# A first expert layer in seven block products per unit, with the products chained in PSUM

## The chip, the core and the metric

The kernel runs on one core of a Trainium2 chip. Five engines work side by side, each through its own instructions in order: TensorE (PE in the profile; its weight loads are PEld), VectorE (DVE), ScalarE (ACT), GpSimd (POOL) and SyncE (SP), which here only issues transfers. The metric is the device time of one execution in microseconds (us), the median of several runs.

## What is computed

Attention with a computed position bias, then a dense layer pair with softplus between, then eight gated experts:

```
x  = attention(q, k, v, bias(w1, b1, w2))            # 1152 tokens x 512
h  = x @ w_in                                        # 512 x 2048, given as float64
x  = (max(h, 0) + log1p(exp(-abs(h)))) @ w_out       # 2048 x 512, float64
P  = exp(x @ w_gate - max); 8 times: normalise rows, then columns
out = sum over e of P[:, e] * (max(x @ w1[e], 0) @ w2[e])   # 8 x (512 x 1024, 1024 x 512)
```

## The kernel before

After the attention the program is a row of 40 *units*. A unit is 256 of the hidden columns of one layer: units 0 to 7 are the dense pair (called the first expert stage here, `u < U1`), units 8 to 39 the eight experts, four units each (the second stage). Every unit does the same work on TensorE, in this order:

- *up*: the 512 x 256 piece of the first matrix against 1024 tokens, the tokens in two blocks of 512 (c = 0, 1), the 256 columns in two blocks of 128 (f = 0, 1), so four results (c, f) of 128 x 512. `up_last` (L763 to L771) does the same for the last 128 tokens.
- the function between the layers (`act`: softplus on ScalarE in the first stage, ReLU in the second), whose result is split into a rounded part `h[:, 0]` (ScalarE) and the rest `h[:, 1]` (VectorE, L736 or L738).
- *down* (L782 to L800): the 256 x 512 piece of the second matrix against the result, for c = 0 in four sums, a pair of transposes (L776), c = 1 in four sums, and one more sum (L809). VectorE adds each sum to the accumulator (L826, or L828 with the gate's weight).

All operands are float32, split in two parts, and each product is three matmuls (`TRIPS`). So the weights of each unit are split as well: `high` (L639) writes the rounded part of the up weights (ScalarE, L636) and the rest (GpSimd, L637), and `highd` (L643) does so for the down weights. The weights of the first stage come as float64 words: four pieces of 128 x 512 in each unit go through `magnitude` (m: a VectorE mask, L601, then a clamp on GpSimd, L602), `convert_a` (a, L607), `convert_b` (b, L612) and `convert_c` (c, L618), on VectorE. The lists `CONVERT` and `JOBS` say at which places of unit u the weights of unit u + 1 are converted, mixed and split; everything goes to the engines in the order in which the Python code names it.

In the second stage (from unit 9) the four up results are not made from eight block products of 128 columns but from seven (`PRODUCTS`), by the Strassen-Winograd scheme: sums of blocks of the tokens (S1 to S4, made once, in unit 8), sums of blocks of the weights (T1 to T4, made by `mix`, L624 to L633, four GpSimd instructions in each unit, then split by a second `high`), seven products, and sums of products on VectorE (`after`, L745 to L761). A block product is six matmuls of 128 x 512 (L699); a plain result of the first stage (`plain`, L702 to L715) is twelve. Units 0 to 8 use `plain`.

PSUM has eight banks: four for the sums of *down* (two tiles of two banks), two under the tag "t", and one each under "tail" and "pv". The gate's small products, in units 8 to 12, take "pv" or "tail" in between (`gate`, asked for at named places).

Of the kernel before, what the change touches and what calls it, by code (L numbers as in the profile page):

```python
# [80 lines left out]
            7: ("S3", "T3")}  # L81
WAT = {"B11": 0, "B21": 512, "B22": 640, "T1": 1024, "T4": 1152, "T3": 1536, "T2": 1664}
# [10 lines left out]
def attention_moe_moe_kernel(ctx: ExitStack, tc, qT, kT, vN, wpos, w_in, w_out, w_gate, e_w1, e_w2,  # L93
# [439 lines left out]
    def experts(m0, accp, xr):  # L533
# [8 lines left out]
        NU = U1 + E * UE  # L542
        wide = w_in.dtype != F32
# [95 lines left out]
        def high(u, k):  # L639
            if u < NU and (u >= U1 or not k):  # L640
# [51 lines left out]
        def product(u, n):  # L692
            z[n] = bank({2: "tail", 5: "pv"}.get(n, "t"))
            xn, wn = PRODUCTS[n]
            k = 0
            for j in range(2):
                for a, b in TRIPS:
                    o = WAT[wn] + 256 * j
                    nc.tensor.matmul(z[n], wu(u)[:, a, o:o + 128], xs[xn][b][j], start=(k == 0), stop=(k == 5))  # L699
# [17 lines left out]
        def add(out, n, name):  # L717
            nc.vector.tensor_tensor(out=out, in0=z[n], in1=hold[name], op=ALU.add)  # L718
# [174 lines left out]
        def tokens_down(c):  # L893
            lt, m = bank("pv"), CHUNKS[c][1] // 128
# [11 lines left out]
        def max_all():  # L906
            mt = bank("pv")
# [3 lines left out]
        def exps():  # L911
            pool["mb"] = mb = bank("pv")
# [16 lines left out]
        def columns(it):  # L929
# [3 lines left out]
            def first():  # L933
                cs["t"] = t = bank("pv")
# [317 lines left out]
```

## Time and profile before

| what | us |
|---|---|
| median of 3 runs (1246.45 to 1248.13) | 1247.13 |
| the profiled execution | 1245.35 |
| its span, first to last instruction | 1243.5 |
| TensorE busy in it | 1186.5 |
| VectorE, GpSimd, ScalarE busy | 825.9, 554.8, 492.4 |

Read with it: the first expert stage lies between 261 and 473 us of the span (unit 1 begins at 295.3, unit 4 at 371.8, unit 5 at 397.3, unit 7 at 448.4), unit 8 ends at 506, and from 608 us on one unit follows another every 23.5 us. A busy TensorE is a modelled figure; how far it waits is read unit by unit, from the length of a unit.

### The profile page before, as it was taken

How to read it: one execution, taken by the hardware profiler on the slowest of the kernel's cores; microseconds unless marked ns; L12 is line 12 of the kernel's file. 1: busy time of each engine (PE TensorE's matmuls, PEld its weight loads, DVE VectorE, ACT ScalarE, POOL GpSimd, SP SyncE). 2: the span in 40 equal slices, each digit the busy share in tenths (PEclk: the TensorE clock that was granted, in tenths of full speed). 3: DMA queues.
4: the chain of work that ended last, by engine and by line, in shares of the span. 5: the costliest groups of instructions: out<-in, count | busy, mean ns of one | idle time of the engine just before them, and what ended most of it. 6: DMA issues, size and time to landing. Idle time of an engine off the chain costs nothing.

```text
span 1243.5 us, 19028 instructions
## 1 busy us (share of the span) xinstructions
PE 1186.5 (95%) x7454; PEld 999.7 (80%) x7454; DVE 825.9 (66%) x1517; ACT 492.4 (40%) x861; POOL 554.8 (45%) x424
## 2 busy tenths in 40 slices
PE   5777899999999999999999999999999999999998
PEld 4776788878788887877888888888888888888887
DVE  8985878746776757467655665655665665665665
ACT  7976677764223334422422322322322322322321
POOL 0115677655445543534444443453453453453440
PEclk9898999999999999999999999999999999999999
DMA  3576565312222310111111111111110111111002
GB/s 102 169 209 201 169 192 174 87 35 85 85 86 85 102 63 22 51 35 35 51 51 35 51 51 35 52 51 35 52 51 34 51 52 35 51 51 35 34 1 76
DMA packets 58572, 90.85 MB, mean 73 GB/s; under 512 B 6900, under 2 KB 37236, under 8 KB 58484
## 3 DMA queue, kind: packets, MB, share of 16 engines
q1 hardware_dynamic: 58196, 89.35, 22.7%
q8 instruction: 58, 0.95, 0.3%
q10 hardware_dynamic: 288, 0.30, 0.1%
q14 instruction: 30, 0.25, 0.1%
HBM read 74.45 MB, written 15.19 MB: 72 GB/s over the span
## 4 chain that ended last, share of the span: by engine, by line
PE 81%; DVE 11%; ACT 2%; POOL 2%; issue 2%; DMA 1%; SPq 0%; POOLq 0%; DVEq 0%
PE sum L793 33%; PE t L699 17%; PE pv L809 4%; PE t L714 4%; PE pv L699 3%; PE tail L699 3%; PE tail L767 3%; PE op L472 3%; PE sps L384 2%; PE tp L435 2%; PE pv L714 2%; PE tail L714 2%; DVE m L200 1%; ACT m L197 1%; PE pac L210 1%
## 5 line engine op out<-in xcount | busy, mean ns | idle before, releaser
L637 POOL TENSOR_TENSOR wu<-f,wu 128x1024 fp32r<-128x1024 f32 x71 | 170.7, 2405 | 439.4 <-ACT wu L636 438.9
L793 PE MATMUL sum<-wd,h 128*128 128x512 f32 x1536 | 365.0, 393 | 0.0
L793 PEld LDWEIGHTS sum<-wd,h 128*128 128x128 f32 x1536 | 283.3, 188 | 56.2
L828 DVE SCALAR_TENSOR_TENSOR acc<-sum,prob,acc 128x512 f32<-128x512 f32 x224 | 168.1, 750 | 137.5 <-PE sum L793 137.5
L699 PE MATMUL t<-room,wu 128*128 128x512 f32 x496 | 137.6, 389 | 0.0
L699 PE MATMUL t<-x,wu 128*128 128x512 f32 x434 | 118.5, 389 | 0.0
L637 POOL TENSOR_TENSOR wd<-f,wd 128x1024 fp32r<-128x1024 f32 x40 | 96.2, 2405 | 40.1 <-ACT wd L636 32.0
L749 ACT ACTIVATE v<-t 128x512 f32<-128x512 f32 x31 | 18.6, 599 | 233.2 <-PE t L699 233.2
L699 PEld LDWEIGHTS t<-room,wu 128*128 128x128 f32 x496 | 93.1, 188 | 19.4
L793 PE MATMUL sum<-h,wd 128*128 128x512 f32 x384 | 93.9, 397 | 1.8 <-DVE acc L826 1.0
L699 PEld LDWEIGHTS t<-x,wu 128*128 128x128 f32 x434 | 81.5, 188 | 16.9
L210 PE MATMUL pac<-bw,m 128*128 128x64 bf16 (+1 forms) x1920 | 67.9, 199 | 28.0 <-ACT m L197 13.3
L210 PEld LDWEIGHTS <-m 128*128 128x128 bf16 (+1 forms) x1920 | 64.5, 105 | 31.3 <-issue 17.9
L793 PEld LDWEIGHTS sum<-h,wd 128*128 128x128 f32 x384 | 69.9, 188 | 20.4 <-DVE acc L826 5.8
L636 ACT ACTIVATE wu<-f 128x1024 fp32r<-128x1024 f32 x71 | 74.8, 1053 | 15.3 <-DVE f L618 15.3
L602 POOL TENSOR_SCALAR f<-f 128x512 f32<-128x512 f32 x32 | 61.6, 1933 | 27.8 <-DVE f L601 27.3
L826 DVE TENSOR_TENSOR acc<-sum,acc 128x512 f32<-128x512 f32 x80 | 55.0, 687 | 23.8 <-PE sum L793 23.0
L718 DVE TENSOR_TENSOR tail<-tail,v 128x512 f32<-128x512 f32 x31 | 21.7, 699 | 68.3 <-PE tail L699 68.3
L734 ACT ACTIVATE hl<-tail 128x256 fp32r<-128x256 f32 x40 | 15.4, 386 | 127.0 <-PE tail L776 127.0
L401 ACT ACTIVATE p<-p,sm 128x576 f32<-128x576 f32 x72 | 55.7, 773 | 23.1 <-DVE sm L397 18.0
L734 ACT ACTIVATE h<-pv 128x512 fp32r<-128x512 f32 x39 | 23.4, 600 | 98.3 <-DVE pv L718 98.1
L734 ACT ACTIVATE h<-t 128x512 fp32r<-128x512 f32 x80 | 47.9, 599 | 35.1 <-DVE t L718 26.8
(196 smaller groups left out, 2157.4 us busy)
## 6 DMA issues: line engine op xcount, KB each, us to landing
f<-in_e_w_dram SPq DMA_DIRECT2D x128, 256.0 KB, 2.8
bias<-wt SPq DMA_DIRECT2D x16, 576.0 KB, 5.5
raw<-in_w_in_dram SPq DMA_DIRECT2D x16, 512.0 KB, 3.6
raw<-in_w_out_dram SPq DMA_DIRECT2D x16, 512.0 KB, 3.6
wt<-extra SPq DMA_DIRECT2D x10, 512.0 KB, 4.8
raw<-in_qT_dram SPq DMA_DIRECT2D x16, 288.0 KB, 4.3
raw<-in_kT_dram SPq DMA_DIRECT2D x16, 288.0 KB, 4.2
vr<-in_vN_dram SPq DMA_DIRECT2D x8, 448.0 KB, 4.7
```

The lines of the kernel that those rows point to most:

```text
L210: nc.tensor.matmul(pt[0:n, g], lhs, win(w, (k * (ng + 1) + gw) * NC, [[(ng - gw) * NC, 2], [1, NC]]), start=(k == 0), stop=(k == 2))
L401: nc.scalar.activation(p, p, AF.Exp, bias=sm[:, o:o + 1], scale=-1.0, accum_out=sm[:, 2 + o:3 + o])
L602: nc.gpsimd.tensor_scalar(t, t, F64_MIN, F64_MAX, ALU.max, ALU.min)
L636: nc.scalar.activation(w[:, 0], src, AF.Copy)
L637: nc.gpsimd.tensor_tensor(out=w[:, 1], in0=src, in1=w[:, 0].bitcast(F32), op=ALU.subtract)
L699: nc.tensor.matmul(z[n], wu(u)[:, a, o:o + 128], xs[xn][b][j], start=(k == 0), stop=(k == 5))
L714: nc.tensor.matmul(zz, wu(u)[:, a, o:o + 128], xs[f"A{c + 1}{k // 2 + 1}"][b][k % 2], start=(k == 0 and n == 0), stop=(k == 3 and n == 2))
L734: nc.scalar.activation(t[:, 0], src, AF.Copy if u < U1 else AF.Relu)
L793: nc.tensor.matmul(s, lhs, rhs, start=(n == 0), stop=(n == 5))
L809: nc.tensor.matmul(r, t[:, b, 128 * f:128 * f + 128], w[:, a, f], start=(n == 0), stop=(n == 5))
L826: nc.vector.tensor_tensor(out=d, in0=o, in1=d, op=ALU.add)
L828: nc.vector.scalar_tensor_tensor(out=d, in0=o, scalar=pool["prob"][:, t, e:e + 1], in1=d, op0=ALU.mult, op1=ALU.add)
```

## The change

- Units 2 to 7 use the seven products as well; units 0, 1 and 8 (`PLAIN`) stay plain. So S1 to S4 of the attention's output are made in units 0 and 1 (`first_plain`, `first_sum`, `first_split`), and `mix` and the second `high` run for units 2 to 7 too.
- In both stages the products run in the order 1, 2, 6, 5, 7, 3, 4, then `up_last` (`UP`), in three banks X ("t"), Y ("tail") and Z ("pv") (`CHAIN`): products 6, 7 and 4 are added to X by TensorE, product 3 to Z. Before X or Z is added to, ScalarE copies it (`keep`: v1 after 1, u2 after 6, u3 after 5). VectorE makes three sums (2, 7, 3) instead of seven; the fourth result is X itself.
- In the first stage the rest of three of the four softplus results is taken on GpSimd, from SBUF (`split_h` with `eng`), and softplus of results 2 and 7 is held back until after products 6 and 4.
- For units 1 to 7 the clamp of the float64 words runs on VectorE.
- The gate's steps are asked for one place later or earlier, some in other banks.

```
 def magnitude(u, k):
-            nc.gpsimd.tensor_scalar(t, t, F64_MIN, F64_MAX, ALU.max, ALU.min)
+            eng = nc.vector if u else nc.gpsimd
+            eng.tensor_scalar(t, t, F64_MIN, F64_MAX, ALU.max, ALU.min)
...
+CHAIN = {1: "X", 2: "Y", 6: "X", 5: "Z", 7: "X", 3: "Z", 4: "X"}
+UP = (1, 2, 6, 5, 7, 3, 4, 0)
...
 def product(u, n):
-            z[n] = bank({2: "tail", 5: "pv"}.get(n, "t"))
+            if n in (1, 2, 5):
+                hold["XYZ"[(1, 2, 5).index(n)]] = bank({1: "t", 2: "tail", 5: "pv"}[n])
+            zz = hold[CHAIN[n]]
...
+        def add(u, bank_, name):
+            out = hold[bank_ if u >= U1 and name != "u3" else name]
+            nc.vector.tensor_tensor(out=out, in0=hold[bank_], in1=hold[name], op=ALU.add)
+            return out
...
+        def keep(name, bank_):
+            hold[name] = pool["moe"].tile([128, 512], F32, tag=name, bufs=1, name=name)
+            nc.scalar.activation(hold[name], hold[bank_], AF.Copy)
...
 def split_h(u, t, src, eng=None):
             nc.scalar.activation(t[:, 0], src, AF.Copy if u < U1 else AF.Relu)
+            if eng:
+                eng.tensor_tensor(out=t[:, 1], in0=src, in1=t[:, 0].bitcast(F32), op=ALU.subtract)
...
 def after(u, n):
+            if n in (1, 6, 5):
+                keep({1: "v1", 6: "u2", 5: "u3"}[n], "Z" if n == 5 else "X")
+            if n in (6, 4):
+                while held:
+                    held.pop(0)()
+            if n in (2, 7, 3, 4):
+                c, f = {2: (0, 0), 7: (1, 1), 3: (0, 1), 4: (1, 0)}[n]
+                z[c, f] = hold["X"] if n == 4 else add(u, *{2: ("Y", "v1"), 7: ("X", "u3"), 3: ("Z", "u2")}[n])
+                low()
...
+                def rest_of():
+                    nc.scalar.activation(z[c, f], hold["X"] if n == 4 else z[c, f], AF.Softplus)
+                    split_h(u, t, z[c, f], None if n == 3 else nc.gpsimd)
...
+        CONVERT0 = "m0 m1 a0 b0 c0 m2 a1 b1 c1 a2 high0 b2 m3 c2 a3 b3 c3".split()
-        CONVERT = "m0 m1 a0 b0 c0 m2 a1 b1 c1 high0 a2 b2 m3 c2 a3 b3 c3 highd0".split()
+        CONVERT = "m0 m1 a0 b0 c0 m2 a1 b1 c1 high0 mix0 a2 b2 m3 c2 a3 high1 b3 c3".split()
...
+                    for n, p in enumerate(UP):
+                        if p:
+                            do(u, p)
+                        else:
+                            up_last(u)
+                        if n == 1:
+                            weights["highd"](u, 0)
+                        if n % 2:
+                            convert(2)
+                        jobs(n)
...
+        def first_sum(name):
+                nc.vector.tensor_tensor(out=t[name][k], in0=a[k], in1=b[k], op=op)
...
+        def first_split(name, eng=nc.gpsimd):
+                nc.scalar.activation(hi, src, AF.Copy)
+                eng.tensor_tensor(out=lo, in0=src, in1=hi.bitcast(F32), op=ALU.subtract)
```

What stands in the engines' rows then. GpSimd in unit 4 of the first stage, before (wu and wd are the up and down weights of unit 5, f a piece on its way there; L602 is the clamp, L637 the rest of a split):

```order
L602 TENSOR_SCALAR f_4602<-f_4602 128x512 x2
L602 TENSOR_SCALAR f_4604<-f_4604 128x512
L637 TENSOR_TENSOR wu_4600<-f_4602,wu_4600 128x1024
L602 TENSOR_SCALAR f_4604<-f_4604 128x512
L637 TENSOR_TENSOR wd_4601<-f_4604,wd_4601 128x1024
```

And now (wd_2554 is unit 4's; h the rests of three results, L750; L634 to L637 the mix for unit 5; L641 the rest of a split):

```order
L641 TENSOR_TENSOR wd_2554<-f_4603,wd_2554 128x1024
L750 TENSOR_TENSOR h<-v_5410,h 128x512
L750 TENSOR_TENSOR h<-u_5445,h 128x512
L750 TENSOR_TENSOR h<-s_5480,h 128x512
L641 TENSOR_TENSOR wu_4600<-f_4602,wu_4600 128x1024
L634 TENSOR_TENSOR f_2556<-f_4602 128x2x2x128
L635 TENSOR_TENSOR f_2556<-f_4602 128x2x128
L636 TENSOR_TENSOR f_2556<-f_4602,f_2556 128x2x128
L637 TENSOR_TENSOR f_2556<-f_2556 128x2x128
L641 TENSOR_TENSOR wu_4600<-f_2556,wu_4600 128x1024
```

The clamps are gone, and the mix, a second split of the up weights and three rests of h came in. VectorE in unit 4 before, from its first row (L601 m, L607 a, L612 b, L618 c, L736 the rest of h):

```order
L601 TENSOR_SCALAR f_4602<-raw_2557 128x512
L601 TENSOR_SCALAR f_4602<-raw_2558 128x512
L736 TENSOR_TENSOR h<-t,h 128x512
L607 TENSOR_SCALAR f_4602<-f_4602 128x512
L612 SCALAR_TENSOR_TENSOR f_4602<-raw_2557,f_4602 128x512
L736 TENSOR_TENSOR h<-t,h 128x512
L618 SCALAR_TENSOR_TENSOR f_4602<-raw_2557,f_4602 128x512
L601 TENSOR_SCALAR f_4604<-raw_4605 128x512
L736 TENSOR_TENSOR h<-tail,h 128x512
L607 TENSOR_SCALAR f_4602<-f_4602 128x512
L612 SCALAR_TENSOR_TENSOR f_4602<-raw_2558,f_4602 128x512
L736 TENSOR_TENSOR h<-pv,h 128x512
```

And now (L606 is the clamp, L727 a sum of products; v is (0, 0), the two u are (1, 1) and (0, 1)):

```order
L727 TENSOR_TENSOR v_5410<-tail,v_5410 128x512
L604 TENSOR_SCALAR f_4602<-raw_2557 128x512
L606 TENSOR_SCALAR f_4602<-f_4602 128x512
L604 TENSOR_SCALAR f_4602<-raw_2558 128x512
L606 TENSOR_SCALAR f_4602<-f_4602 128x512
L611 TENSOR_SCALAR f_4602<-f_4602 128x512
L616 SCALAR_TENSOR_TENSOR f_4602<-raw_2557,f_4602 128x512
L727 TENSOR_TENSOR u_5445<-t,u_5445 128x512
L727 TENSOR_TENSOR u_5433<-pv,u_5433 128x512
L622 SCALAR_TENSOR_TENSOR f_4602<-raw_2557,f_4602 128x512
L604 TENSOR_SCALAR f_4604<-raw_4605 128x512
L606 TENSOR_SCALAR f_4604<-f_4604 128x512
```

Between the first and the second sum of products, the one that reads t (bank X), now stand six conversions. ScalarE at the same place before (L731 softplus, L734 the rounded part of h, L636 that of a weight):

```order
L636 ACTIVATE wd_2554<-f_4603 128x1024
L731 ACTIVATE t<-t 128x512
L734 ACTIVATE h<-t 128x512
L731 ACTIVATE t<-t 128x512
L734 ACTIVATE h<-t 128x512
L731 ACTIVATE tail<-tail 128x512
L734 ACTIVATE h<-tail 128x512
L731 ACTIVATE pv<-pv 128x512
L734 ACTIVATE h<-pv 128x512
```

And now (L732 is a copy of X or Z, L780 softplus, L748 the rounded part of h, L640 that of a weight):

```order
L748 ACTIVATE hl<-tail 128x256
L640 ACTIVATE wu_2553<-f_2556 128x1024
L732 ACTIVATE v_5410<-t 128x512
L640 ACTIVATE wd_2554<-f_4603 128x1024
L732 ACTIVATE u_5433<-t 128x512
L780 ACTIVATE v_5410<-v_5410 128x512
L748 ACTIVATE h<-v_5410 128x512
L732 ACTIVATE u_5445<-pv 128x512
L780 ACTIVATE u_5433<-u_5433 128x512
L748 ACTIVATE h<-u_5433 128x512
L780 ACTIVATE u_5445<-u_5445 128x512
L748 ACTIVATE h<-u_5445 128x512
```

The rounded part of the down weights moved behind the copy v, ahead of the copies u, and both softplus and the rounded parts stand between the copies.

## Rows read from the trace of the kernel before

**Rows 1.** The page: span, then TensorE's busy time, share and instructions.
```profile
span 1243.5 us, 19028 instructions
...
PE 1186.5 (95%) x7454; PEld 999.7 (80%) x7454; DVE 825.9 (66%) x1517; ACT 492.4 (40%) x861; POOL 554.8 (45%) x424
```
**Rows 2.** Busy time by stretch: units 4 and 7, units 9 to 12, unit 13.
```profile
core 0: us, PE busy (x) PEld busy (x) DVE busy (x) ACT busy (x) POOL busy (x), PEclk, DMA share, GB/s
...
371.83:397.34 25.51, 25.31 (x118) 20.60 (x117) 18.64 (x30) 7.62 (x12) 12.40 (x6) 1.00 0.25 83
...
448.35:473.28 24.93, 24.93 (x117) 20.68 (x117) 11.95 (x18) 13.26 (x21) 16.51 (x11) 1.00 0.19 63
...
608.63:632.11 23.48, 23.48 (x112) 19.64 (x111) 14.44 (x21) 6.50 (x10) 10.52 (x7) 1.00 0.13 45
```
**Rows 3.** Chain that ended last, unit 4 into 5: start us, us, what.
```profile
382.71 1.43 PE t L767 x12
384.15 4.12 PE sum L793 x18
...
388.98 1.79 DVE f L607
...
391.43 4.55 PE sum L793 x18
...
397.34 5.44 PE t L714 x24
402.78 2.72 PE tail L714 x12
```
**Rows 4.** Timeline of unit 4: start us, us, engine, line, operation.
```profile
381.32 1.92 POOL L602 TENSOR_SCALAR f<-f 128x512 f32<-128x512 f32 x1 [1.39 <-DVE f L601]
...
381.89 0.42 DVE L607 TENSOR_SCALAR f<-f 128x512 int32<-128x512 int32 x1
...
382.34 0.69 DVE L612 SCALAR_TENSOR_TENSOR f<-raw,f 128x512 int32<-128x512 int32 x1
...
388.10 2.39 POOL L637 TENSOR_TENSOR wu<-f,wu 128x1024 fp32r<-128x1024 f32 x1 [4.86 <-ACT wu L636]
388.29 0.69 DVE L826 TENSOR_TENSOR acc<-sum,acc 128x512 f32<-128x512 f32 x1 [0.67 <-PE sum L793]
388.90 1.88 DVE L607 TENSOR_SCALAR f<-f 128x512 int32<-128x512 int32 x1
```
**Rows 5.** Timeline of the attention, 142 to 149 us, where both engines are dense.
```profile
143.21 3.26 POOL L332 TENSOR_TENSOR ql<-raw,qh 128x576 fp32r<-128x576 f32 x2 [1.58 <-PE sps L384]
...
143.92 1.27 DVE L612 SCALAR_TENSOR_TENSOR f<-raw,f 128x512 int32<-128x512 int32 x1
...
145.22 1.79 DVE L618 SCALAR_TENSOR_TENSOR f<-raw,f 128x512 int32<-128x512 int32 x1
```
**Rows 6.** Groups by line: form and count | busy us, mean ns of one | idle before.
```profile
L637 POOL TENSOR_TENSOR wu<-f,wu 128x1024 fp32r<-128x1024 f32 x71 | 170.7, 2405 | 439.4 <-ACT wu L636 438.9 <-DVE sm L407 0.4
...
L636 ACT ACTIVATE wu<-f 128x1024 fp32r<-128x1024 f32 x71 | 74.8, 1053 | 15.3 <-DVE f L618 15.3
...
L630 POOL TENSOR_TENSOR f<-f 128x512 f32<-128x512 f32 x31 | 40.2, 1296 | 0.0
...
L632 POOL TENSOR_TENSOR f<-f,f 128x256 f32<-128x256 f32 x31 | 23.5, 758 | 0.0
...
L631 POOL TENSOR_TENSOR f<-f 128x256 f32<-128x256 f32 x31 | 23.5, 757 | 0.0
...
L633 POOL TENSOR_TENSOR f<-f 128x256 f32<-128x256 f32 x31 | 23.1, 744 | 0.0
...
L749 ACT ACTIVATE v<-t 128x512 f32<-128x512 f32 x31 | 18.6, 599 | 233.2 <-PE t L699 233.2
...
L660 POOL TENSOR_TENSOR room<-xr,room 128x512 fp32r<-128x512 f32 x6 | 7.7, 1289 | 3.0 <-ACT room L659 2.9
```

More of the change, by code (lines that the diff above doesn't have):

```diff
@@ L542, in experts @@
         NU = U1 + E * UE
+        PLAIN = (0, 1, U1)
         wide = w_in.dtype != F32
@@ L698, in product @@
                     o = WAT[wn] + 256 * j
-                    nc.tensor.matmul(z[n], wu(u)[:, a, o:o + 128], xs[xn][b][j], start=(k == 0), stop=(k == 5))
+                    nc.tensor.matmul(zz, wu(u)[:, a, o:o + 128], xs[xn][b][j], start=(n in (1, 2, 5) and k == 0), stop=(k == 5),
+                                     skip_group_check=True)
                     k += 1
@@ L965, in tokens_max @@
             max_rows()
-        gate = {(0, "a0"): lambda: (tokens_down(1), splits("S3")), (0, "a2"): lambda: logits(2), (0, "b0"): tokens_max,
+        gate = {(0, "a1"): lambda: (tokens_down(1), splits("S3")), (0, "a3"): lambda: logits(2), (0, "b1"): tokens_max,
                 (1, "r1"): max_all, (1, "a0"): exps, (1, "a2"): lambda: rows(pool["prob"], pool["mb"][:, 300:300 + NT]),
@@ L1037, in rest @@
                 load(1, 2 + k)
-            x_part("A22", 0)
-            x_part("A22", 1, nc.vector)
+            for k in range(2):
+                x_part("A22", k, nc.vector)
             for k in range(KT):
@@ L1086, in unit @@
             else:
-                for n, p in enumerate((1, 2, 6, 7, 5, 3, 4)):
-                    do(u, p)
+                for n, p in enumerate(UP):
+                    if n > 4:
+                        ask(u, f"r{n - 5}")
+                    if p:
+                        do(u, p)
+                    else:
+                        up_last(u)
                     jobs(n)
             ask(u, "r0")
-            up_last(u)
+            if u == U1:
+                up_last(u)
             ask(u, "r1")
@@ L1131, in first_up, with first_plain, up @@
             splits("S4")
+        def first_plain():
+            def up(c, f):
+                do(0, (c, f))
+                low()
+                act(0, c, f, z[c, f])
+            tmp = [pool["moe"].tile([128, 512], F32, tag=t, bufs=1, name=t) for t in ("v1", "u2", "u3", "s3")]
+            pool["tmp"] = dict(S1=tmp[0:2], S2=[fs[1][:, 0:512], fs[1][:, 512:1024]], S3=tmp[2:4], S4=tmp[0:2])
+            up(0, 0)
+            first_sum("S1")
+            low()
+            first_sum("S2")
+            up(0, 1)
+            first_split("S1")
+            low()
+            first_sum("S3")
+            up(1, 0)
+            first_sum("S4")
+            up(1, 1)
+            low()
+            convert(5)
+            up_last(0)
+        def first_sum(name):
+            t = pool["tmp"]
+            for k in range(2):
+                a, b, op = {"S1": (x_of("A21"), x_of("A22"), ALU.add), "S2": (t["S1"], x_of("A11"), ALU.subtract),
+                            "S3": (x_of("A11"), x_of("A21"), ALU.subtract), "S4": (x_of("A12"), t["S2"], ALU.subtract)}[name]
+                nc.vector.tensor_tensor(out=t[name][k], in0=a[k], in1=b[k], op=op)
+        def first_split(name, eng=nc.gpsimd):
+            for k in range(2):
+                hi, lo, src = xs[name][0][k], xs[name][1][k], pool["tmp"][name][k]
+                nc.scalar.activation(hi, src, AF.Copy)
+                eng.tensor_tensor(out=lo, in0=src, in1=hi.bitcast(F32), op=ALU.subtract)
         todo = []
```

73 lines of the change are left out of this document (40 added, 33 removed).

## The prediction, made before the run

> **What bounds the kernel now.** I read the page first, for its span and for TensorE's share [rows 1]: 95% busy leaves little to look for elsewhere. Then the busy time by unit [rows 2]. The reader is to see that TensorE sets both stages: a second-stage unit lasts 23.48 us and TensorE is busy for 23.48; the last unit of the first stage, which converts no weights for a successor, lasts 24.93 and TensorE is busy for 24.93. A first-stage unit that does convert lasts 25.51, so it loses 25.51 - 24.93 = 0.58. The chain of waits says to whom [rows 3]: between two stretches of the down sums stands one VectorE conversion, a, for 1.79. The timeline says why [rows 4]: this a took 1.88, where the same instruction takes 0.42, and it began 0.80 after GpSimd's split of the weights and ended 0.29 behind it. An accumulation (one input in PSUM) ran its usual 0.69 inside the same split. So a VectorE instruction that works from SBUF to SBUF with one input stands still until GpSimd's instruction with two SBUF inputs is over. One with two SBUF inputs does too: in the attention [rows 5] b and c took 1.27 and 1.79 instead of 0.69 while GpSimd ran two such instructions in 3.26, and they went in turn, GpSimd, b, GpSimd, c. GpSimd's clamp, with one input, held nobody: a and b ran 0.42 and 0.69 within its 1.92 [rows 4].
>
> **The change part by part.** Times inside a unit count from its first product.
>
> TensorE. Twelve matmuls take 2.72 [rows 3], so a block product of six takes 1.36. Seven in place of eight save 1.36 in each of units 2 to 7: 8.2. Without waits a unit would last 24.93 - 1.36 = 23.57, about what the second stage shows.
>
> GpSimd, in a first-stage unit. It loses four clamps of 1.92, which held nobody. It gains four mix instructions, 1.30 + 0.76 + 0.76 + 0.74 = 3.56, one more split of 2.41, and three rests of h, each taken as the split of 128 x 512 from SBUF, 1.29 [rows 6]. Its time with two SBUF inputs rises from 2 x 2.41 = 4.8 to 3 x 2.41 + 3.56 + 3 x 1.29 = 14.7.
>
> VectorE, in the same unit. The kind that can be held was a, m (0.42 each, both one input) and b, c (0.69): 4 x 2.22 = 8.9. Now four clamps join, a two-operation instruction like a, 0.42, and one rest of h from SBUF, 0.69: 11.3. The new sums of products read PSUM, like the accumulation, and aren't held.
>
> The two add up to 13.7 of 25.51 before, and to 26.0 now. Instructions that follow each other on VectorE start 0.08 before the last one's end [rows 4] (388.29 + 0.69 against 388.90), so the least is 26.0 - 21 x 0.08 = 24.3. That is already more than the 23.57 TensorE wants.
>
> The clamp in rows 4 ran beside a and b. The Trainium skill, page "SBUF — State Buffer", section "Who interferes with whom", says that GpSimd blocks such VectorE instructions for its whole instruction, with no word of one input or two; by it the unit before would already carry 4.8 + 7.7 + 8.9 = 21.4 of 25.51 at a loss of only 0.58, and I would give the first rival below 0.35. The row decides against it.
>
> The loop. What matters is whether one unit's turns end in time for the next. I follow the rows of after, in which each engine works in order, starting where c of piece 1 ends, in down:
> - ScalarE rounds the up weights, GpSimd takes the rest: 1.05 + 2.41 = 3.5.
> - mix, 3.56, in turn with a, b, m and the clamp of pieces 2 and 3: + 0.42 + 0.69 + 0.42 + 0.42 = 5.5.
> - ScalarE rounds the mixed weights (c beside it), GpSimd takes the rest: 3.5.
> - a, b, c of piece 3: 1.8.
> - ScalarE rounds the down weights, GpSimd takes the rest: 3.5. The unit has changed; VectorE evacuates the last sum and makes (0, 0) meanwhile.
> - m, then GpSimd's rest of h, then clamp, m, clamp, a, b: 0.42 + 1.29 + 4 x 0.42 + 0.69 = 4.1.
> - Only now the sum (1, 1), 0.69. It reads X, to which product 4 is to be added.
> - Product 4, up_last and the first down sum: 1.36 + 1.43 + 1.36 = 4.2.
> - Its accumulation, GpSimd's rest of another h, c of piece 1: 0.69 + 1.29 + 0.69 = 2.7.
>
> That is 29.5, less eleven overlaps of 0.08: 28.6, the length of a unit if this chain binds; TensorE then waits some 5 us before product 4. If VectorE got no turns within mix (1.95) and the rest of h stayed out of the last step (1.29) it would be 25.4; with no overlap, and the other rest of h in the way as well, 30.8. I take 28.5, as the turns are what rows 5 show.
>
> - Units 2 to 6: 5 x (28.5 - 25.51) = 15.0, and 0.4 in unit 2 for the late S3.
> - Unit 7 converts nothing, but inherits the late c: this ends 3.5 + 5.5 + 3.5 + 1.8 - 0.6 = 13.7 after the loop's start; the start lies 1.4 + 2.7 = 4.1, less two overlaps 3.9, behind up_last and the next unit 12.2 behind it (nine down sums of 1.36), so c ends 5.4 into unit 7. Two roundings and the copy u2, 2.7, stand between it and product 7, which could start at 4 x 1.36 = 5.4: 2.7 late, less the saved 1.36: +1.3.
> - Unit 1 is still plain, with the mix and the S4 splits for the first time. 1.2 for sums that are accumulated late, between 0 and 2.7 (that rest of h and two of 0.69).
> - Unit 0: eight sums and eight splits more, in a stretch where VectorE has gaps; 0, within 1.5 either way.
>
> Second stage. VectorE makes four sums of 0.69 fewer per unit, off the path, as TensorE is busy for all of a unit [rows 2]: nothing. The new wait is TensorE's for the copies, 0.60 [rows 6]. Each has one product between (1.36), so 0.76 of slack less a hand-over; the sum for X has 0.67. ScalarE is busy 6.50 of 23.48 there. The gate's steps move by a place: 0, within 1.5.
>
> Sum: 15.0 + 0.4 + 1.3 + 1.2 = 17.9. The profiled execution (1245.35, of which 1243.5 is span) would become 1263.3; the median lay 1.8 above it, 1247.13 + 17.9 = 1265.0. I say 1264.
>
> **The rivals.**
> - The turns cost nothing: faster. Place: the sum (1, 1) of units 2 to 6. It decides where that sum ends before product 3 does, at 6 x 1.36 = 8.2 into the unit. For that c of piece 3 must end with the unit before, and both engines need 24.3 of what is then 23.57. Then 8.2 is saved and the 0.58 of units 1 to 6: 1247.1 - 11.7 = 1235. For it: before, 13.7 of 25.51 cost one collision. Against: the loop.
> - The pair binds, but packed: 24.3 and some 1.2 of waiting for ScalarE's roundings, a unit as long as before. 1247, no difference.
> - The copies hold TensorE in the second stage: if u2 comes 0.3 behind its slack in 31 units, 9.3 on top: 1273. Against it ScalarE's idle share.
> - The change doesn't do what it says: the seven products save TensorE's time but no unit gets shorter. That is the forecast's own claim, with the saved time found in waits.
>
> **How the numbers follow.** Forecast (1251 to 1273): 0.66. Turns cost nothing (1232 to 1243): 0.18. Packed (1244 to 1250): 0.08. Copies late (1268 to 1282): 0.08. A measurement here can tell 0.2%, 2.5 us, from no change. Faster: the second case and an edge of the third, 0.20; same 0.06; slower 0.74. The range: nearly all of the forecast, the packed case, the upper half of the fast one and the lower part of the late copies, 1238 to 1274.
>
> **What would show it.** In the profile of after: units 3 to 6 last about 28.5; in the timeline a VectorE m or clamp of about 2.5 lies at GpSimd's split of the down weights, and one beside each mix; TensorE's waits in the first stage are for VectorE's sum (1, 1), several us each; a second-stage unit stays at 23.5. I am wrong if those units last under 25, if VectorE's held instructions show 0.42 and 0.69 beside GpSimd's two-input ones, or if the second stage moves by more than 3.

## The result, and the profile after

The changed kernel takes 1256.33 us (1254.35 to 1256.67, four runs) against 1247.57 for the kernel before in the same comparison: a ratio of 1.0071, 95% interval 1.0058 to 1.0084. It is slower by 8.8 us; 1264 was forecast, in a range of 1238 to 1274. The profiled execution took 1256.67, of which 1254.8 is span, 11.3 more than the span in [rows 1].

The page's totals say little: TensorE's busy time fell by 4.2 and the span grew.

```profile
span 1254.8 us, 18987 instructions
...
PE 1182.3 (94%) x7418; PEld 993.9 (79%) x7418; DVE 809.7 (65%) x1432; ACT 550.2 (44%) x955; POOL 576.9 (46%) x449
```

The busy time by stretch says where, as in [rows 2]. The stretches are units 1, 2, 4, 7, 8, 10 and 13, each from its first product to the next unit's; columns: stretch, length, busy time of each engine with its count, TensorE's granted clock, share and rate of the transfers.

```profile
core 0: us, PE busy (x) PEld busy (x) DVE busy (x) ACT busy (x) POOL busy (x), PEclk, DMA share, GB/s
296.42:326.34 29.92, 27.05 (x118) 21.72 (x116) 26.49 (x35) 11.80 (x20) 18.58 (x12) 0.94 0.23 76
326.34:353.21 26.87, 24.36 (x111) 19.40 (x110) 24.69 (x39) 10.34 (x16) 13.68 (x11) 1.00 0.25 79
380.64:407.93 27.29, 24.36 (x111) 19.39 (x110) 25.12 (x35) 10.10 (x16) 16.36 (x11) 1.00 0.24 78
462.76:488.60 25.84, 24.81 (x112) 19.23 (x110) 16.14 (x20) 14.61 (x24) 23.24 (x15) 1.00 0.19 64
488.60:520.38 31.78, 31.07 (x154) 23.63 (x153) 19.93 (x35) 15.41 (x27) 10.93 (x8) 1.00 0.10 34
544.85:569.14 24.29, 24.29 (x118) 20.30 (x116) 15.94 (x41) 7.78 (x12) 10.52 (x7) 1.00 0.13 44
617.18:640.65 23.47, 23.47 (x111) 19.62 (x110) 12.31 (x17) 7.76 (x12) 10.48 (x7) 1.00 0.15 46
```

And three of them in the kernel before, which the forecast had no rows for (units 1, 8 and 10):

```profile
295.18:320.64 25.46, 25.31 (x118) 20.60 (x116) 17.00 (x27) 7.71 (x13) 12.40 (x6) 1.00 0.24 81
473.12:506.22 33.10, 31.32 (x155) 23.58 (x153) 19.91 (x35) 15.53 (x27) 10.74 (x8) 1.00 0.10 32
530.82:556.25 25.43, 24.93 (x117) 20.06 (x116) 18.30 (x45) 6.50 (x10) 10.49 (x7) 1.00 0.13 42
```

So unit 1 grew by 4.5. Units 2 to 6 grew by 1.3, 1.9, 1.8, 2.0 and 1.9, together 8.9, and unit 7 by 0.9. Unit 8 shrank by 1.3, units 9 to 12 by 2.7 in all, and from unit 13 on nothing moved: 23.47 as in [rows 2]. Unit 1 began 1.2 later. That adds up to 11.4.

In units 2 to 6 TensorE is busy for about 24.4, where the forecast had 23.57 and unit 13, with the same products, has 23.47; it stands for nearly 3. What the 0.9 more of busy time is made of is open, but for a part: the first matmul behind the wait takes 0.50 instead of 0.39. The chain of work that ended last in unit 4 (start us, us, what) runs along VectorE through nearly the whole unit, where [rows 3] had TensorE with one VectorE piece of 1.79:

```profile
386.01 2.51 DVE f L606
388.52 1.44 DVE f L604
...
391.39 0.70 DVE u L727
...
392.13 1.65 PE t L706 x6
...
396.64 0.69 DVE acc L853
397.34 1.42 DVE f L622
```

L604 is the mask m, L606 the clamp, L622 the step c; L727 at 391.39 is the sum (1, 1). The timeline of GpSimd in the same stretch gives the reason for the clamp of 2.51 and the m of 1.44 (0.42 each when nothing holds them):

```profile
385.62 2.62 POOL L641 TENSOR_TENSOR wd<-f,wd 128x1024 fp32r<-128x1024 f32 x1 [2.44 <-ACT wd L640]
388.19 1.48 POOL L750 TENSOR_TENSOR h<-v,h 128x512 fp32r<-128x512 f32 x1
```

Both end 0.3 behind a GpSimd instruction with two SBUF inputs (385.62 + 2.62 = 388.24, 388.19 + 1.48 = 389.67), as the a in [rows 4] did. The c stands beside the next rest of h. What TensorE waited for in units 2 to 7 (waited for: us, times, longest):

```profile
PE t L706 <- DVE u L727: 12.3, 5, 2.7
PE pv L706 <- DVE acc L853: 2.0, 6, 0.8
```

Those are the five waits before product 4 for the sum (1, 1), 1.7 in unit 2 and 2.6 to 2.7 in units 3 to 6, and six short ones before product 5 for the bank that the last accumulation still reads.

### The profile page after: what moved, and what is told of

Same layout as the page of the kernel before. It is cut to its first block, busy times and chain, and to the rows that moved or that the text cites. A ratio compares the mean times of both kernels' runs of the same rounds, so it can differ in the third digit from the quotient of the medians.

```text
span 1254.8 us, 18987 instructions
## 1 busy us (share of the span) xinstructions
PE 1182.3 (94%) x7418; PEld 993.9 (79%) x7418; DVE 809.7 (65%) x1432; ACT 550.2 (44%) x955; POOL 576.9 (46%) x449
## 4 chain that ended last, share of the span: by engine, by line
PE 72%; DVE 19%; ACT 3%; issue 2%; POOL 2%; DMA 1%; SPq 0%; POOLq 0%; DVEq 0%; ACTq 0%
PE sum L820 31%; PE t L706 14%; PE pv L706 7%; PE tail L794 4%; PE pv L836 3%; PE tail L706 3%; PE op L474 3%; DVE f L616 2%; DVE acc L853 2%; DVE f L622 2%; DVE f L606 2%; PE sps L386 2%; PE tp L437 2%; DVE f L604 1%; ACT m L199 1%
## 5 line engine op out<-in xcount | busy, mean ns | idle before, releaser
L641 POOL TENSOR_TENSOR wu<-f,wu 128x1024 fp32r<-128x1024 f32 x77 | 186.4, 2421 | 432.1 <-ACT wu L640 431.7
L706 PE MATMUL t<-room,wu 128*128 128x512 f32 x592 | 165.2, 391 | 12.5 <-DVE u L727 12.3
L706 PEld LDWEIGHTS t<-room,wu 128*128 128x128 f32 x592 | 111.0, 188 | 38.3 <-DVE u L727 14.4
L732 ACT ACTIVATE v<-t 128x512 f32<-128x512 f32 x37 | 22.2, 599 | 244.2 <-PE t L706 244.2
L706 PE MATMUL pv<-x,wu 128*128 128x512 f32 x444 | 114.0, 392 | 2.0 <-DVE acc L853 2.0
L641 POOL TENSOR_TENSOR wd<-f,wd 128x1024 fp32r<-128x1024 f32 x40 | 97.1, 2427 | 29.7 <-ACT wd L640 25.6
L640 ACT ACTIVATE wu<-f 128x1024 fp32r<-128x1024 f32 x77 | 81.0, 1052 | 45.0 <-POOL f L637 28.2
L706 PEld LDWEIGHTS pv<-x,wu 128*128 128x128 f32 x444 | 82.5, 188 | 21.9 <-DVE acc L853 4.5
L706 PE MATMUL t<-x,wu 128*128 128x512 f32 x296 | 85.2, 389 | 0.0
L748 ACT ACTIVATE hl<-tail 128x256 fp32r<-128x256 f32 x40 | 15.4, 386 | 143.0 <-PE tail L803 143.0
L853 DVE TENSOR_TENSOR acc<-sum,acc 128x512 f32<-128x512 f32 x80 | 54.9, 686 | 24.2 <-PE sum L820 23.7
L727 DVE TENSOR_TENSOR u<-t,u 128x512 f32<-128x512 f32 x37 | 25.5, 690 | 66.3 <-PE t L706 66.3
L727 DVE TENSOR_TENSOR tail<-tail,v 128x512 f32<-128x512 f32 x31 | 21.7, 699 | 67.4 <-PE tail L706 67.4
L706 PEld LDWEIGHTS t<-x,wu 128*128 128x128 f32 x296 | 55.6, 188 | 11.4
```

The lines of the kernel that those rows point to most:

```text
L640: nc.scalar.activation(w[:, 0], src, AF.Copy)
L641: nc.gpsimd.tensor_tensor(out=w[:, 1], in0=src, in1=w[:, 0].bitcast(F32), op=ALU.subtract)
L706: nc.tensor.matmul(zz, wu(u)[:, a, o:o + 128], xs[xn][b][j], start=(n in (1, 2, 5) and k == 0), stop=(k == 5), skip_group_check=True)
L727: nc.vector.tensor_tensor(out=out, in0=hold[bank_], in1=hold[name], op=ALU.add)
L853: nc.vector.tensor_tensor(out=d, in0=o, in1=d, op=ALU.add)
```

## The experiments

Each is named by its label. "Before" in a result is the kernel before in the same comparison.

### The second stage alone, and the gate's places

e1_second_stage_only is the kernel before with the new `product`, `add`, `keep`, `after` and `UP` for units 9 to 39 only, and the gate's banks and places of the change; units 0 to 8 stay plain.

```
+CHAIN = {1: "X", 2: "Y", 6: "X", 5: "Z", 7: "X", 3: "Z", 4: "X"}
+UP = (1, 2, 6, 5, 7, 3, 4, 0)
...
-                for n, p in enumerate((1, 2, 6, 7, 5, 3, 4)):
+                for n, p in enumerate(UP):
+                    if n > 4:
+                        ask(u, f"r{n - 5}")
```

> The kernel before with the second stage of the change alone: products chained in X, Y and Z, ScalarE copies, gate steps in their new places and banks; units 0 to 8 plain, clamp on GpSimd. Theory: the 4.0 us that units 8 to 12 lost between the two profiles (33.10 to 31.79, and 24.60, 25.43, 25.43, 24.06 to 24.46, 24.29, 24.29, 23.75) come from the second stage's own changes: 1247.6 - 4.0 = 1243.6. Rival, the forecast's own step (the second stage is worth nothing, and those units only gained because the first stage ended differently): 1247.6 within 1.

1241.86 against 1246.69, ratio 0.9965 (0.9953 to 0.9978): 4.8 faster. Its units 8 and 10 last 31.79 and 24.29, as in the change, and units 1 to 7 are those of before. So the second stage's part of the change is a gain, and the first stage's part costs 8.8 + 4.8 = 13.6, if the two add up.

e6_gate_old_places takes that kernel and asks for the gate's steps where the kernel before asked.

```
-        gate = {(0, "a1"): lambda: (tokens_down(1), splits("S3")), (0, "a3"): lambda: logits(2), (0, "b1"): tokens_max,
+        gate = {(0, "a0"): lambda: (tokens_down(1), splits("S3")), (0, "a2"): lambda: logits(2), (0, "b0"): tokens_max,
...
-                    if n > 4:
-                        ask(u, f"r{n - 5}")
+                    if not p:
+                        ask(u, "r0")
```

> The second stage's change alone (the chained products, the gate in its new banks), with the gate's steps asked for at the places of the kernel before: its first row step behind product 4, the two others behind the last rows, the steps in unit 8 one place earlier. Theory (the 4.8 us came from the places: TensorE meets each gate product a step later or earlier, when VectorE is done): back to between 1245 and 1247. Rival (they came from the banks and the shorter VectorE work between products): it stays at 1242.

1246.94 against 1246.34, ratio 1.0004 (0.9995 to 1.0013): the gain is gone. The waits of TensorE (waited for: us, times, longest) say how; first this kernel's from unit 8 to unit 10, then those of e1_second_stage_only:

```profile
PE tail L902 <- ACT acc L830: 2.0, 1, 2.0
PE tail L902 <- DVE hl L750: 0.8, 1, 0.8
PE t L942 <- DVE prob L932: 0.6, 1, 0.6
```
```profile
PE tail L902 <- ACT acc L830: 0.7, 1, 0.7
```

The gate's small products stand in TensorE's queue like any other. Its transposes in unit 8 (L902) wait here for what stands ahead of them on ScalarE and VectorE; in the change they stand a place later, when most of that is done. The column sum that waits in unit 10 (L942) stands at the same place in both kernels. What moved is the step that makes its input: in the change the gate's steps beside the up products of units 9 to 12 come two places earlier.

The zero is a sum of two things. Units 9 to 12 last 98.2 in all (99.5 in the kernel before, 96.8 in e1_second_stage_only), so there half of the gain stays. Unit 8 lasts 35.56, 2.5 longer than before, and its granted clock was 0.95: TensorE is busy for 32.78 of it, against 31.10 in e1_second_stage_only, so 1.7 is the clock's. The places' own share is therefore not exactly the 4.8. The old banks at the new places were not tried, so the banks' share is open too.

### Does GpSimd's second input hold VectorE?

e2_clamp_gpsimd undoes the clamp.

```
-                eng = nc.vector if u else nc.gpsimd
+                eng = nc.gpsimd
```

> The changed kernel with the float64 clamp on GpSimd again in every unit. Theory (GpSimd holds VectorE only while it runs an instruction with two SBUF inputs; the clamp has one): VectorE loses 4 x 0.43, GpSimd gains 4 x 1.92 that hold nobody, but the clamp of piece 3 now queues behind the mix, 0.9 ahead of the second up split: units 2 to 6 between 27.0 and 28.3 (27.3 now), total 1255 to 1262. Rival (GpSimd holds VectorE in any instruction): 4 x (1.92 - 0.43) = 6.0 more per unit, 33, total above 1280.

1267.62, ratio 1.0183 (1.0159 to 1.0207). Units 4 and 6 last 28.2, within what was expected; units 3 and 5 last 29.8 at a granted clock of 0.94, and unit 1 32.5, which was not. So the total lies 5.6 above the upper end, and 12 below the rival's. The timeline shows VectorE's b at 0.69, its usual time, inside GpSimd's two clamps:

```profile
393.91 3.97 POOL L606 TENSOR_SCALAR f<-f 128x512 f32<-128x512 f32 x2
...
396.89 0.69 DVE L616 SCALAR_TENSOR_TENSOR f<-raw,f 128x512 int32<-128x512 int32 x1
```

The a ahead of it (396.03) took 0.82 instead of 0.42: it began together with the second clamp. So the clamp costs VectorE 0.4 at most there, and not its whole length.

e12_two_input_clamp asks the same the other way round. It stands on the fastest kernel below (e9_stage2_half_rests, plain first stage).

```
-                nc.gpsimd.tensor_scalar(t, t, F64_MIN, F64_MAX, ALU.max, ALU.min)
+                if u < 2:
+                    nc.gpsimd.tensor_scalar(t, t, F64_MIN, F64_MAX, ALU.max, ALU.min)
+                    return
+                for n, op in enumerate((ALU.mult, ALU.mult)):
+                    nc.gpsimd.tensor_tensor(out=t, in0=t, in1=pool["lim"][:, n:n + 1].to_broadcast([128, 512]), op=op)
...
+            pool["lim"] = mp.tile([128, 2], F32, name="lim")
...
```

> The run with the plain first stage and the rests in halves (1238.8), in which GpSimd's clamp of the float64 words in units 2 to 7 (one instruction with one SBUF input, 1.92) is replaced by two instructions with two SBUF inputs each, a multiplication by one of 1.3 (the clamp is left out there). Theory (GpSimd holds VectorE in an instruction with two SBUF inputs, not in one with one): beside these, VectorE's m, a, b and c show holds of 1.3 to 1.7 where they now show 0.42 to 0.82, three or more in each of units 2 to 6; the units get longer where a held instruction stands ahead of an accumulation, 24.9 to 25.5, total 1239 to 1243. Rival (what holds VectorE is the large transfer of the split, or its writes of rounded values, not the second input): no such holds beside them, units 24.9, total 1238 to 1239.

The same two conversions (a, then b) beside GpSimd, first in e9_stage2_half_rests with the clamp, then with the multiplications (timelines of unit 4):

```profile
377.02 3.81 POOL L604 TENSOR_SCALAR f<-f 128x512 f32<-128x512 f32 x2
378.97 0.82 DVE L609 TENSOR_SCALAR f<-f 128x512 int32<-128x512 int32 x1 [1.71 <-POOL f L604]
379.83 0.69 DVE L614 SCALAR_TENSOR_TENSOR f<-raw,f 128x512 int32<-128x512 int32 x1
```
```profile
376.86 4.34 POOL L608 TENSOR_TENSOR f<-f,lim 128x512 f32<-128x512 f32 x4
379.05 1.25 DVE L613 TENSOR_SCALAR f<-f 128x512 int32<-128x512 int32 x1 [2.01 <-POOL f L608]
380.33 1.41 DVE L618 SCALAR_TENSOR_TENSOR f<-raw,f 128x512 int32<-128x512 int32 x1
```

b takes 1.41 instead of 0.69, a 1.25 instead of 0.82, beside instructions that are shorter one by one (1.1) than the clamp. Five such holds stand in unit 4. The expected mechanism holds, though the held instructions are a little shorter than put (0.9 to 1.4). Every GpSimd instruction that held VectorE in these runs is a TENSOR_TENSOR, and the one that didn't is a TENSOR_SCALAR; whether the second input counts or the operation, no run here separates. The Trainium skill, page "SBUF — State Buffer", section "Who interferes with whom", says that the engine that comes first keeps the shared ports for its whole instruction; the trace agrees for GpSimd's instructions with two inputs, and not for the clamp. The total, 1254.42, is 11 above the expected range and says nothing on this: the second-stage units, whose code is the same, lengthened from 23.47 to 23.7 and 24.0 (last section). Units 2 to 6 last 25.5 to 25.7, and TensorE is busy for all of that, so these holds cost it no wait.

e10_half_rests cuts GpSimd's rest of the weights in two.

```
-            nc.gpsimd.tensor_tensor(out=w[:, 1], in0=src, in1=w[:, 0].bitcast(F32), op=ALU.subtract)
+            for a in (0, 512):
+                nc.gpsimd.tensor_tensor(out=w[:, 1, a:a + 512], in0=src[:, a:a + 512], in1=w[:, 0, a:a + 512].bitcast(F32), op=ALU.subtract)
```

> The changed kernel with GpSimd's rest of the weights in two instructions of 128 x 512. Theory (one turn each): in units 3 to 6 the longest held VectorE instruction falls from 2.77 to about 1.7, but as many conversions as before stand between, now each held once, so the sum (1, 1) is no earlier: units 27 to 27.8, total 1254 to 1259. Rival (the length of one hold is what costs): units below 26.5, total below 1252. If VectorE is held until GpSimd is idle, holds stay at 2.6 or longer.

1254.21, ratio 1.0058 (1.0044 to 1.0071). The longest held instruction now takes 1.66. Where a clamp and an m took 2.51 and 1.44, three instructions are held for one turn each:

```profile
384.17 1.41 DVE L606 TENSOR_SCALAR f<-f 128x512 f32<-128x512 f32 x1
385.50 1.51 DVE L604 TENSOR_SCALAR f<-raw 128x512 int32<-128x512 int32 x1
387.05 1.39 DVE L606 TENSOR_SCALAR f<-f 128x512 f32<-128x512 f32 x1
```

The sum (1, 1) came no earlier, and TensorE's wait before product 4 is 2.47 to 2.76. Unit 6, at full clock, lasts 26.95; units 3 to 5 last 28.1 to 28.4 at a granted clock of 0.94. What was won (2.1 in the total) lies in unit 1 (27.72), unit 7 (25.02) and unit 8 (31.06). Most of unit 1's 2.2 is the clock, which didn't fall there: TensorE is busy for 25.18 of it, against 27.05 in the changed kernel.

### The first stage's loop

e3_sum_first moves four conversion steps behind the sum (1, 1).

```
-                        if n % 2:
-                            convert(2)
+                        convert({4: 4, 5: 2, 7: 2}.get(n, 0))
```

> The changed kernel with one change of order: in units 2 to 7 the four conversion steps that VectorE was given ahead of the sum (1, 1) are given behind it. Theory (the loop runs through the place of that sum in VectorE's queue, behind six conversions of which two are held by GpSimd): the wait of 2.63 before product 4 goes, units 2 to 6 last 24.8 instead of 27.3, total 1256.3 - 5 x 2.5 = 1244. Rival (VectorE and GpSimd together are full whatever the order, 26.0 of turns): the wait turns up elsewhere, at the mixed weights or at the accumulations, units 26 or longer, total 1250 to 1256.

1248.95 against 1246.69, ratio 1.0018 (1.0009 to 1.0028): of the 8.8 lost, 2.3 are left. The wait before product 4 is gone, and units 3 to 6 last 25.9. Neither 24.8 nor "26 or longer" is quite it: the wait went, a smaller one came, 0.88 in the first down sum for the rounded part of (0, 1), whose sum now stands behind the conversions:

```profile
391.26 0.50 PE L820 MATMUL sum<-h,wd 128*128 128x512 f32 x1 [0.88 <-ACT h L748]
391.99 2.33 PE L820 MATMUL sum<-h,wd 128*128 128x512 f32 x9 [0.23 <-DVE h L752]
```

e4_results_in_psum takes two rests of h off GpSimd.

```
-            out = hold[bank_ if u >= U1 and name != "u3" else name]
+            out = hold[bank_ if name != "u3" else name]
...
-                if n == 4:
-                    z[c, f] = pool["moe"].tile([128, 512], F32, tag="s3", bufs=1, name="s3")
...
-                    nc.scalar.activation(z[c, f], hold["X"] if n == 4 else z[c, f], AF.Softplus)
-                    split_h(u, t, z[c, f], None if n == 3 else nc.gpsimd)
+                    nc.scalar.activation(z[c, f], z[c, f], AF.Softplus)
+                    split_h(u, t, z[c, f], nc.gpsimd if n == 7 else None)
```

> The changed kernel with three of the four first-stage results kept in PSUM (results of products 2, 3 and 4), and their rests taken on VectorE from PSUM; only the rest of (1, 1) stays on GpSimd. Theory (VectorE waits out GpSimd's two-input instructions): GpSimd has two rests of 1.3 to 1.5 less per unit, so the m beside the first of them (1.51) and the c beside the second (1.50) fall to 0.42 and 0.69, and units 2 to 6 from 27.3 to about 25.5; total 1256.3 - 5 x 1.8 = 1247. Rival (the rests hold nobody, and the two long instructions have another reason): VectorE has 0.69 more to do twice, nothing is won, 1256 to 1260.

1253.45, ratio 1.0052 (1.0038 to 1.0065). The m and the c beside those rests fell to 0.41 and 0.68, as the theory has it, but the clamp kept its 2.52, and TensorE's wait before product 4 only fell from 2.63 to 2.1 and 2.4. Units 4 and 6 last 26.2 and 26.1; units 3 and 5 last 28.2 and 28.3. The difference between these is mostly the clock. TensorE behind the wait in unit 3, then in unit 4 (stretch, length, busy, granted clock):

```profile
361.60:363.00 1.40, 1.40 (x3) 0.50 0.00 0
...
389.40:390.00 0.60, 0.60 (x3) 1.00 0.00 0
```

0.50 of 2.4 GHz is the lower level, 1.2. TensorE's busy time for the same matmuls was 25.66 in unit 3 and 24.08 in unit 4, so that fall cost 1.6.

e7_loop_reordered is the loop laid out by hand.

```
-                            weights["highd"](u, 0)
-                        if n % 2:
-                            convert(2)
+                            nc.scalar.activation(wd(u)[:, 0], whole2(u, 1), AF.Copy)
+                        if n == 2:
+                            nc.gpsimd.tensor_tensor(out=wd(u)[:, 1], in0=whole2(u, 1), in1=wd(u)[:, 0].bitcast(F32), op=ALU.subtract)
+                        convert({1: 4, 5: 2, 7: 3}.get(n, 0))
...
-            if n in (6, 4):
+            if n in (6, 3):
...
-                convert(len(todo))
+                convert(len(todo) - (2 if 0 < u < U1 - 1 else 0))
...
                 down_last(u)
+                convert(len(todo))
```

> The changed kernel with the first-stage loop laid out again for units 2 to 7, the same instructions: GpSimd takes the rest of h (0, 0) before the rest of the down weights; the four conversion steps ahead of the sum (1, 1) stay, none stands ahead of the sum (0, 1); the softplus of (1, 1) goes ahead of that of (0, 1); b and c of piece 3 go behind the last accumulation. Theory (each wait of the first stage is a place in a queue; the conversions then run while GpSimd is idle): the waits before product 4 and in the first down sum go, units 2 to 6 about 24.5 (27.3 in the change, 25.9 with the sum moved alone), total 1256.3 - 5 x 2.8 = 1242. Rival (the two engines' turns fill a unit of 26 in any order): units 25.9 or longer, total 1248 or more.

1256.06, ratio 1.0076 (1.0060 to 1.0091): nothing was won; units 4 to 6, at full clock, last 27.2 to 27.4. The wait before product 4 is gone here too, but GpSimd's rests now lie beside the steps between the sum (0, 1) and its rest, and hold all three; TensorE waits 2.05 in the first down sum:

```profile
364.57 1.65 DVE L622 SCALAR_TENSOR_TENSOR f<-raw,f 128x512 int32<-128x512 int32 x1
366.14 1.52 DVE L604 TENSOR_SCALAR f<-raw 128x512 int32<-128x512 int32 x1
367.69 1.37 DVE L606 TENSOR_SCALAR f<-f 128x512 f32<-128x512 f32 x1
...
369.71 2.50 PE L820 MATMUL sum<-h,wd 128*128 128x512 f32 x5 [2.05 <-DVE h L752]
```

e8_mask_on_scalar takes the mask off VectorE. It stands on e3_sum_first; the masks for two pieces each are asked for behind the fourth and the last step of `UP`.

```
-                nc.vector.tensor_scalar(t.bitcast(I32), words(u, k)[:, :, 1], 0x7FFFFFFF, None, ALU.bitwise_and)
+                if u < 2:
+                    nc.vector.tensor_scalar(t.bitcast(I32), words(u, k)[:, :, 1], 0x7FFFFFFF, None, ALU.bitwise_and)
...
+                if 2 <= u < U1 and wide:
+                    nc.scalar.activation(whole(u, k), words(u, k)[:, :, 1].bitcast(F32), AF.Abs)
```

> The run with the sum (1, 1) moved ahead of four conversion steps, and in addition the sign mask m of the float64 words of units 2 to 7 taken on ScalarE (absolute value) instead of VectorE, issued ahead of its clamp. Theory (what is left in the units of 25.9 is VectorE's queue between the sum (1, 1) and the first accumulation: (0, 1) comes 1.1 late and the third down sum waits): VectorE has three times 0.42 less there; units 2 to 6 from 25.9 to about 24.8, unit 1 from 30.0 to 28.5; total 1249 - 7 = 1242. Rival (GpSimd's own chain of rests and mix sets 25.9): units stay at 25.5 or more, total 1246 to 1249.

1260.16, ratio 1.0105 (1.0091 to 1.0119): theory and rival both missed a cost. Between softplus and absolute value ScalarE loads a table, four times in a unit:

```profile
390.14 1.28 ACT L612 ACT_TABLE_LOAD   x1
391.43 1.22 ACT L612 ACTIVATE f<-raw 128x512 f32<-128x512 f32 x2
392.68 1.28 ACT L786 ACT_TABLE_LOAD   x1
```

The copies and roundings come late for it, and units 3 to 6 last 28.4. The run doesn't test what it was made for.

e11_sums_first_half_rests joins e3_sum_first and e10_half_rests, with two steps instead of four between the sums.

```
-                        convert({4: 4, 5: 2, 7: 2}.get(n, 0))
+                        convert({4: 2, 5: 2, 7: 2}.get(n, 0))
```

> The change with all that helped so far in the first stage: the sum (1, 1) ahead of the conversions, only two conversion steps (instead of four) between it and the sum (0, 1), and GpSimd's rests of the weights in halves. Theory (the seven products can be had if no queue stands in the way): the waits of 0.88 and 0.27 of the first of these runs go, units 2 to 6 from 25.9 to about 25.0, unit 1 to 27.7 and unit 8 to 31.1 as with the halves alone; total 1249 - 4.5 - 2.2 - 0.7 = 1241.6, which still doesn't reach the 1238.8 of the plain first stage with halves. Rival (VectorE and GpSimd fill the unit, and what is taken from one wait comes back in the next): units 25.7 or longer, total 1245 or more. It beats 1238.8 only if units 2 to 6 come to 24.4.

1259.22, ratio 1.0110 (1.0094 to 1.0125). The rival holds: the steps that were moved back now stand behind the accumulations, so the up weights of the next unit are split later, the mix is later, and TensorE waits for the mixed weights (units 2 to 7; waited for: us, times, longest):

```profile
PE t L707 <- POOL wu L642: 10.6, 5, 2.1
```

Units 4 and 6 last 27.8, and 3 and 5, at a clock of 0.94, 29.4.

### Unit 1

e5_s4_later moves the rests of S4.

```
-                            first_split("S4")
...
                 turn_last(u)
+                if u == 1:
+                    first_split("S4", nc.vector)
                 down(u, 1)
```

> The changed kernel with one move in unit 1: the two rests of S4 run on VectorE between the two down halves instead of on GpSimd behind the split of the down weights. Theory (unit 1 lost 4.5 because those rests, 1.75 and 1.74, hold a c and an m on VectorE, 1.18 and 1.51 instead of 0.69 and 0.42, so that the accumulation and with it TensorE's third down sum come late): the wait of 2.13 falls to about 0.5; unit 1 from 29.9 to 28.3, and to 26.7 if TensorE's granted clock, 0.50 for some 3 us behind that wait, then stays at 1.00; total 1253 to 1254.7. Rival (the b held for 2.84 by the split itself sets it): the wait stays at 1.5 or more, the clock falls as before, total 1255.5 to 1257.

1256.25 against 1246.34, ratio 1.0087 (1.0072 to 1.0101): no gain. The wait of 2.13 for an accumulation did fall to 0.52, the c and the m to 0.68 and 0.41. But one of 1.86 came in the other half, where S4's rests on VectorE are held in their turn by the mix (1.45 and 1.21) ahead of an accumulation. Both kernels lose the clock behind their long wait. The changed kernel's (TensorE: stretch, length, busy, granted clock):

```profile
314.85:316.00 1.15, 1.15 (x5) 0.93 0.00 0
316.00:319.00 3.00, 3.00 (x9) 0.50 0.52 175
```

That part of unit 1's price is read from the busy times: 27.05 against 25.31 for the same matmuls, 1.7 of the 4.5. The e10_half_rests run agrees: its unit 1 waits for 2.5 at the same place, the clock stays at 1.00 and TensorE is busy for 25.18.

### A version that beats both

e9_stage2_half_rests is e1_second_stage_only with the edit of e10_half_rests.

> The second stage's change alone (1241.9) with GpSimd's rest of the weights taken in two instructions of 128 x 512 instead of one of 128 x 1024. Theory (VectorE is held until GpSimd's present instruction ends, and then has its turn): the a that costs units 1 to 6 0.58 each is held 1.3 at most instead of 1.88; units 1 to 6 from 25.5 to about 25.0, total 1241.9 - 3 = 1239. Rival (VectorE is held until GpSimd has nothing more to do): a is held as long as before, GpSimd takes 0.17 more, total 1242 to 1243.

1238.77 against 1246.78, ratio 0.9935 (0.9922 to 0.9949). The a that cost units 1 to 6 0.58 each ([rows 3], 1.79) is down to 0.78, and TensorE is busy for all of a unit (unit 4, columns as in the first table of stretches):

```profile
372.40:397.30 24.90, 24.90 (x117) 20.68 (x116) 18.02 (x31) 7.62 (x12) 12.89 (x8) 1.00 0.28 85
```

It is 8.0 faster than the kernel before, where the changed kernel is 8.8 slower. It has the change's second stage, no seven products in the first, and GpSimd's long instruction cut in two.

## Why the prediction came out as it did

The direction and the mechanism were right, the range holds the time, and 1264 is 8 too high. The loop was put too high, the second stage's gain was taken for nothing, and unit 1 was put too low. That the three partly cancel is luck.

- **The loop: right in kind, 15.4 became 8.9.** The forecast's steps were measured in unit 4 and on into unit 5, from ScalarE's rounding of the down weights to the next, 27.3 long:

```profile
384.48 1.06 ACT L640 ACTIVATE wd<-f 128x1024 fp32r<-128x1024 f32 x1 [1.68 <-DVE f L622]
...
411.82 1.06 ACT L640 ACTIVATE wd<-f 128x1024 fp32r<-128x1024 f32 x1 [1.73 <-DVE f L622]
```

In order: rounding and rest 3.8 (3.5 was forecast), from there to the sum (1, 1) 3.1 (4.1), the sum 0.7, product 4 to the first down sum 4.5 (4.2), its accumulation and c 2.1 (2.7), rounding and rest 3.6 (3.5), mix 4.4 (5.5), rounding and rest 3.8 (3.5), and what is left of b and c 1.3 (1.8). The failing sentence is "the turns are what rows 5 show". There VectorE's held instructions follow each other. Beside the mix the accumulations stand between them, which nothing holds, so a conversion comes up when GpSimd's instruction is nearly over: each is held for a few tenths, and GpSimd gives up 0.8 in all (4.4 - 3.56) and not 1.95. That is read from the timeline, and no run tests it apart. A b beside the mix (0.69 when nothing holds it) and the instruction of the mix that follows (0.76 alone):

```profile
402.27 1.48 POOL L634 TENSOR_TENSOR f<-f 128x512 f32<-128x512 f32 x1
403.45 0.85 DVE L616 SCALAR_TENSOR_TENSOR f<-raw,f 128x512 int32<-128x512 int32 x1
403.71 1.20 POOL L635 TENSOR_TENSOR f<-f 128x256 f32<-128x256 f32 x1
```

So the sign "one beside each mix" for an m or clamp of about 2.5 did not come; the one at the split of the down weights did (2.51). The forecast's other bound, 25.4, had the turns at nothing; the value lay between.
- **The first rival, turns that cost nothing, is out:** it asked for a sum (1, 1) that ends before product 3 does, and in the trace TensorE waits for it in five units, up to 2.7. e4_results_in_psum and e12_two_input_clamp show the holds come and go with GpSimd's two-input instructions.
- **The packed rival** (a unit as long as before, 25.5) isn't what the change does, but e3_sum_first comes near it with 25.9. No order that was tried reached the 24.3 that was worked out as the least. That nothing could is not shown.
- **Unit 1: 1.2 became 4.5.** I priced sums that are accumulated late, 0 to 2.7, and TensorE's waits are that size (0.7 and 2.1). Left out was what the clock takes behind a wait, 1.7. The forecast had no term for that anywhere.
- **Unit 7: 1.3 became 0.9**, near enough.
- **The second stage: 0, within 1.5, became -4.0 in the profiles and -4.8 in the timed runs.** More than 3 was the forecast's own sign of being wrong there. "The gate's steps move by a place" was put down as nothing, since TensorE is busy for all of a unit [rows 2]. That was read from unit 13, which has no gate. Unit 10 of the kernel before lasts 25.43 with TensorE busy for 24.93, and unit 8 lasts 33.10 with 31.32; the forecast took units 9 to 12 as one stretch and didn't ask for what TensorE stood there. What the gate's products wait for was in the trace of the kernel before (units 9 to 12):

```profile
PE pv L936 <- DVE prob L926: 0.8, 2, 0.4
```

- **The copies of the second stage** cost nothing, as forecast: units from 13 on last 23.47 as before.
- **Unit 0: 0 became 1.2**, within its 1.5. In the runs that leave the attention and unit 0 as in the change, unit 1 begins between 293.9 and 297.7, so the term can't be told from the scatter of executions.

## What to carry to other kernels

Before work is moved to GpSimd to spare VectorE, count its instructions with two SBUF inputs: each puts VectorE's SBUF-to-SBUF work into turns, and a queue that runs in order passes the hold on to whatever stands behind, here the sum that TensorE needed. Cutting a long one in two cost GpSimd some 0.2 here and took 3.1 off the total where the hold stood on the path (e9_stage2_half_rests against e1_second_stage_only); in the seven-product loop it left the wait as it was. And read the units that differ from the pattern (here those with the gate) for themselves; a saving or a loss sits there that the common unit doesn't show.

## What the runs showed of the hardware

- A wait of TensorE can cost more than its length. Behind some waits of 1.9 to 3.2 the granted clock fell to 0.50 (1.2 GHz) for some 3 us, once for 6. By the busy time of the same matmuls that cost 1.0 to 2.1 each time, and 2.5 that once (unit 5 of e5_s4_later). Behind others, up to 3.06 long (units 4 and 6 of e2_clamp_gpsimd), it stayed at 1.00. In the profiled execution of the changed kernel the four waits of 2.6 to 2.7 before product 4 went without; in that of e5_s4_later, whose units 3 to 6 are the same code and wait 2.6 to 2.7 at the same place, the clock fell in all four (0.94, 0.94, 0.88 and 0.94 over the unit, 28.2 to 29.7 long instead of 27.4); that execution took 1260.28, the three others of the same kernel 1256.1 to 1256.3. So one profile doesn't give the price of a wait to better than 2 us. What decides is open.
- ScalarE's table load took 1.28 at each change between softplus and absolute value, while softplus and copies alternate without one. The Trainium skill, page "ScalarE: Activation LUTs", section "What ACT_TABLE_LOAD costs", gives 1283 ns for the load itself; the trace agrees (1.28).
- In e12_two_input_clamp one new tile of 8 bytes in each partition was allocated ahead of the others. TensorE's second-stage matmuls of 128 x 512 then took 394 ns on average instead of 389, in units whose code hadn't changed. That the place of the operands in SBUF makes the difference is argued, not shown; it wasn't tried apart.
